# Two phase sums per group moved from ahead of the sixth to ahead of the seventh block product, from the fourth group on

## The chip, the core and the metric

The kernel runs on one core of a Trainium2 chip. The metric is the device time of one execution in microseconds (us). A run is measured as the median of its executions; one further execution is recorded by the hardware profiler, and all views of the profile below are of that one.

## What is computed

Two layers follow each other. The first is a recurrence with a complex gate per channel, over 4 batches, 8 heads, 768 steps and 48 channels; the second multiplies each of the 3072 rows by a 384 x 2048 matrix, applies h * cos(h), and multiplies by a 2048 x 384 matrix.

```python
mag = np.sqrt(a_re * a_re + a_im * a_im)
scale = np.minimum(mag, 0.999) / (mag + 1e-06)
a_re_n, a_im_n = (a_re * scale, a_im * scale)
for t in range(S):
    new_re = ar * S_re - ai * S_im          # ar, ai: gate of step t
    new_im = ar * S_im + ai * S_re
    kv = np.einsum('bhd,bhe->bhde', k[:, :, t], v[:, :, t])
    S_re, S_im = (new_re + kv, new_im)
    y[:, :, t] = np.einsum('bhd,bhde->bhe', q[:, :, t], S_re)
...
h = x @ w_in                                # x: y with the heads side by side
g = h * np.cos(h)
return (g @ w_out).astype(np.float32)
```

## The kernel before

The 768 steps of a batch are cut into 6 chunks of 128 steps, and two chunks make a group, so that there are 12 groups (0 to 11) of 256 rows. Within a chunk the recurrence becomes ordinary matrix products: the gates' magnitudes and angles are summed up along the chunk, the keys and queries are scaled by the exponentials of the sums and turned by the sines and cosines of the summed angles, and then scores, masked scores times values, and a running state give y. Summed-up angles are called phases here.

From group 2 on the function fast_path writes out one round per group n, a loop at L1541. A round mixes work of three groups. Of group n it does the scores and y (chunks, L1243), the transport of y through DRAM into the layout xT (f_x and f_xt, L1031 and L1040), and the first half of the second layer (first, L1253: eight tiles hp of two matmul groups each, with cosine and product behind each). Of group n - 1 it does the second half of the second layer. Of group n + 1 it prepares keys and queries: prods (L1226), phases (L1240) and keys (L1209).

The second half of the second layer is done, from group 2 on, by a scheme of seven block products in place of eight (seventh, L1149). Each product is eight matmuls of 128 x 192, in two parts of four. The first, fourth, sixth and seventh products add into one PSUM tile, sum, which has a single buffer; the second, third and fifth go to tiles op. After the first product ScalarE copies sum out (L1170), after the fourth VectorE adds it to an output tile (L1175), after the sixth ScalarE copies it out again, and after the seventh ScalarE copies it a last time. All these results are collected in the tiles ot. The next product that writes sum has to wait until the copy or addition of the one before has read it.

The phases of a group are two calls of g_phase (L870). Together they are six matmuls of 128 x 384 with operands hi and lo, which split the angle in two parts. Behind each call ScalarE rounds the result to whole turns (a cast to int32) and VectorE subtracts it. The step g_trig (L884) then takes two sines on ScalarE, and g_stack (L897) forms the stacked keys ks and queries qs by four products on VectorE. f_transpose (L909) transposes each in blocks of 32 on VectorE (tr), writes it to DRAM (moved, L921), and reads it back as kT by four DMAs (L924) or as qT by one (L926). The transpose of the queries is held behind the round's first gate product (gated, L919). kT and qT are what the scores of the next round read.

The order within a round is not written out. The function weave (L1196) gets lists of steps, each list with two bounds between 0 and 1; it spreads a list's steps evenly over its stretch and then runs all steps in the order of their places. TensorE's instructions are chained in exactly that order (matmul, L688), and so are the ScalarE activations that go through special and the guards on GpSimd; the remaining VectorE and ScalarE instructions and the SP queue's DMAs get their order from a scheduling layer that goes by readiness and by that same sequence. Each engine then works off its instructions in order, and all DMAs that matter here are issued from the SP queue, also in order.

With the bounds of the kernel before, the eight parts of the fourth to seventh products (products(n - 1, 3, 7), 0.4 to 0.56) stand at 0.41, 0.43 and so on to 0.55; the sixth product has 0.49 and 0.51, the seventh 0.53 and 0.55. The two phases stand at 0.473 and 0.475. keys has four steps at 0.515 (g_trig), 0.545 (g_stack and p_end), 0.575 (transpose of the keys) and 0.605 (transpose of the queries). The eight steps of first begin at 0.5875 and are 0.055 apart.

Of the kernel before, what the change touches and what calls it, by code (L numbers as in the profile page):

```python
# [487 lines left out]
def fast_path(ctx, tc, q, k, v, a_re, a_im, moe_w_in, moe_w_out, out, least, odd, wide):  # L488
# [171 lines left out]
    def behind(ins, other):  # L660
        tc.add_manual_dep(ins.ins, other.ins.name, mybir.DependencyInfo(
            mybir.DependencyClass.NoSync, mybir.DependencyReason.DATA))
# [54 lines left out]
    def spans(g):  # L717

        return [(i, 1) for i in range(G)] if g == 0 else [(0, G)]
# [116 lines left out]
    def p_end(g, i, n):  # L836
        end = X[g]["end"][:, ds(i * H, n * H)]
        vector.tensor_scalar(out=end, in0=end, scalar1=-0.5, scalar2=None, op0=ALU.mult)
        low = least[:, ds(i * H, n * H)]
        vector.scalar_tensor_tensor(out=low, in0=end, scalar=LEAST, in1=low,  # L840
                                    op0=ALU.is_ge, op1=ALU.min)
# [28 lines left out]
    def g_phase(g, i):  # L870

        x, n = X[g], g * G + i
        ps = pa.tile([C, DM], F32, tag="a", name="phs")
        early = g < PEG and n % NCH
        if not early:
            summed_up(ps, g, i, "tan", turns[0])
        else:
            matmul(ps, lhsT=turns[0], rhs=cut(x["tan"], i, 1), start=True, stop=False)
            matmul(ps, lhsT=last, rhs=before(n), start=False, stop=True)
        ph = cut(x["tan"], i, 1)  # L880
        scalar.copy(out=ph.bitcast(I32), in_=ps)
        vector.tensor_tensor(out=ph, in0=ps, in1=ph.bitcast(I32), op=ALU.subtract)

    def g_trig(g, i, n):  # L884
        x = X[g]
        if i == 0:
            x["cos"] = temp("rs")
            if g:
                x["sin"] = temp("lo")
        cs, sn = cut(x["cos"], i, n), cut(x["sin"], i, n)  # L890
        ph = cut(x["tan"], i, n)
        vector.tensor_scalar(out=cs.bitcast(U32), in0=ph.bitcast(U32),
                                scalar1=0x7FFFFFFF, scalar2=None, op0=ALU.bitwise_and)
        special(out=sn, in_=ph, func=AF.Sin, scale=TWO_PI)
        special(out=cs, in_=cs, func=AF.Sin, scale=-TWO_PI, bias=half_pi_b)

    def g_stack(g, i, n):  # L897
        x = X[g]
        if i == 0:
            for name in "ks", "qs":  # L900
                x[name] = gt.tile([C, G * H, 2, D], F32, tag=name, name=name)
        for name, product in ("ks", "Q"), ("qs", "mag"):
            for a, trig in enumerate(("cos", "sin")):
                vector.tensor_tensor(
                    out=x[name][:, ds(i * H, n * H), a],
                    in0=cut(x[product], i, n).rearrange("p (x d) -> p x d", d=D),
                    in1=cut(x[trig], i, n).rearrange("p (x d) -> p x d", d=D), op=ALU.mult)

    def f_transpose(g, i, n, name):  # L909


        if i == 0:
            X[g][name] = ft.tile([D2, G * H, Q4, 32] if name == "kT" else [D2, Q4, G * H, 32], F32,
                                 tag=name, name=name, bufs=1)
        tr = ft.tile([C, NB, n * H, 32], F32, tag="tr", name="tr")
        turn = vector.transpose(out=tr, in_=X[g][name[0] + "s"][:, ds(i * H, n * H)].rearrange(
            "p x a d -> p x (a d)").rearrange("p x (r b) -> p b x r", b=NB))
        if name == "qT" and "gated" in X[g - 1]:
            behind(turn, X[g - 1]["gated"])  # L919
        moved = rows_d.tile([Q4, D2, n * H, 32], F32, tag="moved", name="moved", bufs=3)  # L920
        nc.sync.dma_start(out=moved.rearrange("q (r b) x j -> (q r) b x j", b=NB), in_=tr)  # L921
        if name == "kT":
            for q4 in range(Q4):
                nc.sync.dma_start(out=X[g][name][:, ds(i * H, n * H), q4], in_=moved[q4])  # L924
        else:
            nc.sync.dma_start(out=X[g][name][:, :, ds(i * H, n * H)],  # L926
                              in_=moved.rearrange("q c x j -> c q x j"))
# [178 lines left out]
    PLAIN, HJ, E2 = 2, NJ // 2, DM // 2  # L1106
# [4 lines left out]
    def quarters():  # L1111

        for name in "s1", "s2", "a22":
            right[name] = stage["pool"].tile([C, HJ, E2], F32, name="t_" + name)
        t1, t2, t4 = (right[name] for name in ("s1", "s2", "a22"))
        for j in range(0, HJ, 2):
            for t, a, b in (t1, b12, b11), (t2, b22, t1), (t4, b21, t2):
                yield lambda t=t, a=a, b=b, j=j: behind(vector.tensor_tensor(
                    out=t[:, ds(j, 2)], in0=a[:, ds(j, 2)], in1=b[:, ds(j, 2)],
                    op=ALU.subtract), Y[PLAIN * G]["masked"])  # L1120

    def last_quarter():

        for j in range(0, HJ, 2):
            yield lambda j=j: vector.tensor_tensor(
                out=b12[:, ds(j, 2)], in0=b22[:, ds(j, 2)], in1=b12[:, ds(j, 2)],
                op=ALU.subtract)
# [59 lines left out]
    def products(g, lo, hi):  # L1187
        if g < PLAIN:
            return []
        return [lambda p=p, part=part: seventh(g, p, part)  # L1190
                for p in range(lo, hi) for part in range(2)]

    def mixes(g, lo, hi):
        return [lambda p=p: mixed(g, p) for p in range(lo, hi)] if g >= PLAIN else []

    def weave(*parts):  # L1196

        items = []
        for p, (part, lo, hi) in enumerate(parts):
            part = list(part)  # L1200
            items += [(lo + (hi - lo) * (i + 0.5) / len(part), p, t)
                      for i, t in enumerate(part)]
        for _, _, t in sorted(items, key=lambda x: x[:2]):
            t()
# [4 lines left out]
    def keys(g):  # L1209

        if not 0 <= g < NG:
            return
        for i, n in spans(g):
            yield lambda i=i, n=n: g_trig(g, i, n)
            yield lambda i=i, n=n: (g_stack(g, i, n), p_end(g, i, n))
            for name in "kT", "qT":
                if g >= PEG:
                    yield lambda i=i, n=n, name=name: f_transpose(g, i, n, name)
# [7 lines left out]
    def prods(g):  # L1226
        if not 0 <= g < NG:
            return
        if g not in (1, 2):
            yield from powers(g)  # L1230
            yield lambda: g_angle(g, 0, G)
        yield lambda: (g_carry(g), g_split(g))
        yield lambda: (p_even(g, 0, G), p_apply(g, 0, G))

    def logs(g):
        yield from each(g_log, g)
        if 0 <= g and g + 1 < NG:
            yield lambda: load(g + 1, ("re", "im"))

    def phases(g):  # L1240
        return [lambda i=i: g_phase(g, i) for i in range(G)] if 0 <= g < NG else []

    def chunks(g):  # L1243
        for n in range(g * G, g * G + G):
            for hh in range(2):
                yield lambda n=n, hh=hh: f_scores(n, hh)
            yield lambda n=n: f_state(n)
            yield lambda n=n: f_out(n)
        yield lambda: (f_x(g), f_xt(g))
        if g + 2 < NG:  # L1250
            yield lambda: load(g + 2, ("k", "q", "v"))

    def first(g):  # L1253
        order = range(NJ // 2) if g < PLAIN else (0, 4, 1, 5, 2, 6, 3, 7)
        return [lambda jp=jp: mm1(g, jp) for jp in order]

    def second(g, i):
        return [lambda j0=j0: mm2(g, i, j0, 4) for j0 in range(0, NJ, 4)] if g < PLAIN else []
# [282 lines left out]
    for n in range(2, NG):  # L1541
        weave((mixes(n - 1, 2, 4), 0.0, 0.12), (logs(n + 1), 0.0, 0.02), (chunks(n), 0.0, 0.36),
              (upper[2:] if n == 2 else [], 0.0, 0.2), (products(n - 1, 0, 3), 0.0, 0.36),
              (prods(n + 1), 0.25, 0.27), (second(n - 1, 1), 0.36, 0.5),
              (products(n - 1, 3, 7), 0.4, 0.56), (phases(n + 1), 0.472, 0.476),
              (keys(n + 1), 0.5, 0.62), (quarters() if n == PLAIN else [], 0.4, 0.9),
              (last_quarter() if n == PLAIN else [], 0.9, 1.0), (first(n), 0.56, 1.0),
              (mixes(n, 0, 2), 0.9, 1.0), (guarded(n - 1, per) if n > 3 else [], 0.1, 0.9))
    weave((mixes(NG - 1, 2, 4), 0.0, 0.1), (products(NG - 1, 0, 7), 0.0, 1.0))
# [76 lines left out]
```

## Time and profile before

| What | us |
|---|---|
| median of 3 runs | 666.53 |
| lowest and highest of them | 664.78 and 667.04 |
| the profiled execution's own time | 666.49 |
| its span, from the first to the last instruction | 664.7 |
| TensorE busy within it | 644.0 |
| VectorE busy | 491.7 |
| ScalarE busy | 393.3 |

The span lacks what lies before the first and after the last instruction, 1.8 us. In the views a line of a timeline gives start and length in us, engine, source line, operation, tiles (what is written, an arrow, what is read), shape, the number of instructions merged into it, and in brackets the idle time of the engine just ahead of it with the one that ended it. PE is TensorE's matmuls, PEld its weight loads, which overlap them; DVE is VectorE, ACT ScalarE, SPq the SP queue, whose lines are issues of DMAs and not the transfers. Every matmul shows up twice in the counts of such lines (x16 is a product of eight matmuls in fp32), and almost all carry the helper's line L689, so the tiles tell them apart: phs is a phase, sum and op the block products, hp the first half of the second layer, sc the scores. A row of the view of waits gives who waited for whom, the sum in us, the number of times, and the longest.

A round of groups 3 to 10 takes 51.0 to 52.3 us from one pair of phases to the next.

### The profile page before, as it was taken

To read this page: it belongs to the slowest core of one execution; us is meant where nothing else is said; L and a number is where in the kernel's file an instruction comes from. 1 tells how busy PE (TensorE), PEld (TensorE's weight loads), DVE (VectorE), ACT (ScalarE), POOL (GpSimd) and SP (SyncE) were. 2 spreads that over 40 slices of the span, in tenths; PEclk is the share of its full clock that TensorE was granted. 3 is DMA by queue.
4 is the path that set the end of the run, shared out by engine and by line. 5 is a ranking of instruction groups with operands and counts; after the bars stand their busy time and mean duration, and the time that the engine had idled before them with its cause. 6 is when DMAs were issued, how large, how long until landed. Compare 5 with 4: busy or idle time off the path is not lost.

```text
span 664.7 us, 10764 instructions
## 1 busy us (share of the span) xinstructions
PE 644.0 (97%) x4077; PEld 575.7 (87%) x4077; DVE 491.7 (74%) x797; ACT 393.3 (59%) x728; POOL 28.0 (4%) x47
## 2 busy tenths in 40 slices
PE   7899999999999999999999999999999999999995
PEld 5788867767998999899899899898899899899895
DVE  4999989499788688688688688687688778762241
ACT  7888687284673593593594494495486486332330
POOL 2010200000000000010010010000000000000000
PEclk9999999999999999999999999999999999999998
DMA  9968755637628557657648637826927833533000
GB/s 245 207 190 215 211 170 120 166 64 186 132 48 209 124 145 190 143 139 170 166 126 188 164 100 163 214 72 146 240 80 164 206 94 96 164 98 96 25 6 25
DMA packets 233626, 94.90 MB, mean 143 GB/s; under 512 B 208846, under 2 KB 222033, under 8 KB 233564
## 3 DMA queue, kind: packets, MB, share of 16 engines
q1 hardware_dynamic: 227068, 68.62, 45.2%
q0 software_dynamic: 5632, 25.17, 11.4%
q8 instruction: 34, 0.56, 0.4%
q10 hardware_dynamic: 864, 0.33, 0.2%
q14 instruction: 28, 0.23, 0.1%
HBM read 69.28 MB, written 24.81 MB: 142 GB/s over the span
## 4 chain that ended last, share of the span: by engine, by line
PE 83%; DMA 5%; ACT 5%; DVE 5%; issue 1%; POOL 0%; DVEq 0%; SPq 0%; POOLq 0%
PE hp L689 37%; PE op L689 17%; PE sum L689 11%; PE sc L689 5%; PE yp L689 5%; PE sp L689 4%; DMA xT<-x 2%; PE phs L689 2%; DMA raw<-in_moe_w_out_dram 1%; ACT rs L709 1%; DVE tan L678 1%; PE lgs L689 1%; DVE mag L678 1%; ACT lo L709 1%; DMA x<-yT 1%
## 5 line engine op out<-in xcount | busy, mean ns | idle before, releaser
L689 PE MATMUL hp<-xT,w_in 128*128 128x256 f32 (+1 forms) x1176 | 252.7, 375 | 1.4 <-DMA xT<-x 1.4
L689 PEld LDWEIGHTS hp<-xT,w_in 128*128 128x128 f32 x1176 | 219.5, 190 | 32.2 <-DMA xT<-x 2.0
L709 ACT ACTIVATE gate<-hp,half_pi_b 128x512 f32<-128x512 f32 x96 | 66.0, 687 | 120.5 <-PE hp L689 120.5
L678 DVE TENSOR_TENSOR gate<-hp,gate 128x512 f32<-128x512 f32 x96 | 65.8, 685 | 70.3 <-ACT junk L678 69.8
L689 PE MATMUL op<-w_out,gate 128*128 128x192 f32 (+1 forms) x448 | 100.7, 374 | 0.0
L689 PEld LDWEIGHTS op<-w_out,gate 128*128 128x128 f32 x448 | 75.9, 190 | 16.9 <-issue 2.0
L678 ACT ACTIVATE junk<-hp 128x512 bf16<-128x512 f32 x96 | 56.6, 590 | 0.0
L689 PE MATMUL sum<-t_s,s 128*128 128x192 f32 x320 | 55.4, 326 | 0.2 <-DVE ot L678 0.2
L678 DVE TENSOR_TENSOR atm<-sc,causal 128x512 f32<-128x512 f32 x48 | 32.8, 687 | 30.0 <-PE sc L689 30.0
L689 PEld LDWEIGHTS sum<-t_s,s 128*128 128x128 f32 x320 | 52.6, 190 | 0.5 <-DVE ot L678 0.5
L689 PEld LDWEIGHTS sc<-qT,kT 96*128 96x128 f32 x384 | 47.7, 192 | 1.9 <-ACT qT L678 0.5
L689 PE MATMUL sc<-qT,kT 96*128 96x128 f32 x384 | 49.0, 275 | 0.2 <-ACT qT L678 0.2
L678 ACT ACTIVATE ot<-sum 128x192 f32<-128x192 f32 x30 | 9.5, 319 | 45.8 <-PE sum L689 45.8
L689 PE MATMUL yp<-atm,v 128*48 128x128 f32 x352 | 33.6, 277 | 1.1 <-DVE atm L678 1.1
L705 ACT ACT_TABLE_LOAD x24 | 30.8, 1283 | 4.0 <-DMA ident<-ident_const 3.6
L678 ACT CAST tan<-phs 128x384 int32<-128x384 f32 x24 | 11.4, 480 | 36.5 <-PE phs L689 36.5
L689 PE MATMUL sum<-w_out,s 128*128 128x192 f32 x144 | 25.8, 332 | 4.2 <-ACT ot L678 4.2
L689 PEld LDWEIGHTS sp<-v,ks 128*96 128x96 f32 x320 | 29.7, 165 | 0.0
L689 PE MATMUL yp<-qT,state 96*48 96x128 f32 x304 | 29.7, 272 | 0.0
L689 PE MATMUL sp<-v,ks 128*96 128x48 f32 x320 | 29.7, 245 | 0.0
L689 PE MATMUL sum<-w_out,gate 128*128 128x192 f32 x160 | 29.6, 329 | 0.0
L689 PEld LDWEIGHTS sum<-w_out,s 128*128 128x128 f32 x144 | 23.1, 190 | 6.9 <-ACT ot L678 6.9
(138 smaller groups left out, 976.2 us busy)
## 6 DMA issues: line engine op xcount, KB each, us to landing
moved<-tr SPq DMA_DIRECT2D x20, 768.0 KB
raw<-in_moe_w_in_dram POOLq DMA_DIRECT2D x16, 768.0 KB, 5.3
raw<-in_moe_w_out_dram POOLq DMA_DIRECT2D x16, 768.0 KB, 4.9
kT<-moved SPq DMA_DIRECT2D x40, 192.0 KB
qT<-moved SPq DMA_DIRECT2D x10, 768.0 KB
k<-in_k_dram SPq DMA_DIRECT2D x24, 192.0 KB
q<-in_q_dram SPq DMA_DIRECT2D x24, 192.0 KB
v<-in_v_dram SPq DMA_DIRECT2D x24, 192.0 KB
```

The lines of the kernel that those rows point to most:

```text
L678: ins = getattr(self.engine, op)(**kw)
L689: chain(nc.tensor.matmul(out, **kw), "tensor")
L705: chain(nc.scalar.preload_act_table_set(table))
L709: chain(nc.scalar.activation(func=func, **kw))
```

## The change

In every round but that of group 2 (PLAIN is 2), the two phases of group n + 1 get the bounds 0.516 to 0.524 in place of 0.472 to 0.476, and its keys 0.53 to 0.64 in place of 0.5 to 0.62.

```diff
-              (products(n - 1, 3, 7), 0.4, 0.56), (phases(n + 1), 0.472, 0.476),
-              (keys(n + 1), 0.5, 0.62), (quarters() if n == PLAIN else [], 0.4, 0.9),
+              (products(n - 1, 3, 7), 0.4, 0.56),
+              (phases(n + 1), *((0.472, 0.476) if n == PLAIN else (0.516, 0.524))),
+              (keys(n + 1), *((0.5, 0.62) if n == PLAIN else (0.53, 0.64))),
+              (quarters() if n == PLAIN else [], 0.4, 0.9),
```

The phases then stand at 0.518 and 0.522, between the second part of the sixth product and the first part of the seventh, where they stood between the fifth and the sixth. The steps of keys come to 0.544, 0.571, 0.599 and 0.626: g_trig between the two parts of the seventh product, g_stack behind it, and the two transposes between the first and the second tile of the first layer half.

In the built program this changes eight rounds, n = 3 to 10; the round of group 11 has no further group to prepare. On TensorE only the six phase matmuls and the eight of the sixth product change places. On ScalarE the copy of sum after the sixth product moves from behind the two sines to ahead of the two casts. On VectorE the addition of op after the sixth product moves from behind the two products ks to ahead of the two phase subtractions, and in some of the rounds a small scaling, end, goes ahead of the transpose of the keys. On the SP queue the order is the same except in round 10, where the moved of the queries is issued ahead of the four kT instead of behind them. No instruction is added or removed.

## The prediction

> **What bounds the kernel now.** The page first. Its first section says that TensorE decides, and so does the chain that ended last (83% PE).
>
> ```profile
> PE 644.0 (97%) x4077; PEld 575.7 (87%) x4077; DVE 491.7 (74%) x797; ACT 393.3 (59%) x728; POOL 28.0 (4%) x47
> PEclk9999999999999999999999999999999999999998
> ```
>
> The granted clock is full throughout (0.996 in the mean), so only two things can change the time: TensorE's work, which the edit leaves alone, and TensorE's pauses. The view of waits lists those, for weight loads in the window 190:590:
>
> ```profile
> PEld sum L689 <- ACT ot L678: 6.2, 8, 0.8
> PEld lgs L689 <- DVE lo L678: 1.3, 3, 0.5
> PEld sum L689 <- DVE ot L678: 0.5, 1, 0.5
> PEld hp L689 <- DMA xT<-x: 0.5, 1, 0.5
> ```
>
> Eight waits of 0.77 us (6.2 / 8) are by far the largest item, one in each of the eight rounds n = 3 to 10 that the edit touches. Next I read one round, n = 4, in the timelines of TensorE, ScalarE, VectorE and the SP queue:
>
> ```profile
> 253.35 0.34 PE L689 MATMUL phs<-lo,exact 128*128 128x384 f32 x1
> 253.52 2.76 PE L689 MATMUL sum<-t_s,s 128*128 128x192 f32 x16
> 256.76 2.87 PE L689 MATMUL sum<-w_out,s 128*128 128x192 f32 x16 [0.48 <-ACT ot L678]
> 259.47 20.88 PE L689 MATMUL hp<-xT,w_in 128*128 128x256 f32 x96
> 280.19 1.06 PE L689 MATMUL sc<-qT,kT 96*128 96x128 f32 x8
> ...
> 256.40 0.31 ACT L678 ACTIVATE ot<-sum 128x192 f32<-128x192 f32 x1
> ...
> 250.86 0.35 DVE L678 SCALAR_TENSOR_TENSOR ot<-sum,ot 128x192 f32<-128x192 f32 x1
> 259.53 2.25 DVE L678 STREAM_TRANSPOSE tr<-ks 128x1536 f32<-128x1536 f32 x1
> 263.56 0.69 DVE L678 TENSOR_TENSOR gate<-hp,gate 128x512 f32<-128x512 f32 x1 [1.73 <-ACT junk L678]
> 264.16 2.24 DVE L678 STREAM_TRANSPOSE tr<-qs 128x1536 f32<-128x1536 f32 x1
> ...
> 261.80 4.96 SPq L921 DMA_DIRECT2D moved<-tr  x2
> 266.85 4.62 SPq L924 DMA_DIRECT2D kT<-moved  x4
> 271.58 2.66 SPq L926 DMA_DIRECT2D qT<-moved  x1
> ```
>
> Line 2 is the sixth product (eight matmuls), line 3 the seventh. Both accumulate in the same tile, sum. ScalarE copies it out between them, and TensorE stands still until that copy ends at 256.71. The phases stand just ahead of the sixth product. Below it, the path that starts at the phases: transposes on VectorE, seven DMAs on SP, and the scores of the next round at 280.19.
>
> **What the Trainium skill says.** "PSUM — Partial Sum Buffer", section "PSUM bank collisions raise a hardware error": the hardware does not hold one engine back while another uses the bank, so the program must wait. The trace agrees: the copy ends at 256.71 and the seventh product starts at 256.76. "Perfetto Trace Analysis", section "Tensor Engine Instruction (MATMUL, LD_WEIGHTS)": ScalarE and VectorE are strict FIFO, so a copy waits for all that is queued ahead of it. The trace agrees: the copy follows the sine rs (255.58 + 0.92 us) with no gap. "DMA: Bandwidth & Descriptors", section "Two DMAs through the same engine are not ordered": a DMA that reads what another wrote must wait for its completion on the issuing engine. Here this is why SP strings moved, kT and qT one behind the other.
>
> **The change part by part.** *The stall that goes.* Weight loads show the step: the sixth product's first load is at 253.35, the first load of hp at 259.31, 5.96 us apart. Two products with no pause take 2 x 2.60 (247.28 to 249.88 is one). So a round loses 0.76 us; eight rounds lose 6.0. Afterwards the six phase matmuls (252.64 + 1.06 in the chain of waits) stand in the gap. The copy starts about 0.1 us after the last matmul's modelled end, some 0.3 us into the phases, and takes 0.31: it is done with about 0.3 us to spare, and ScalarE has nothing before it (idle 3.52 us ahead of the casts). In ScalarE's new order the copy is ahead of the casts. I take the whole 0.76.
>
> *The cover that goes.* The phases now hide another read of the same tile: VectorE adds the fourth product's sum (ot<-sum,ot) before the sixth may overwrite it. Without them the sixth product wants its weights where the first phase load stands today. In rounds 4, 6, 7, 9, 10 that read ends 0.6 to 1.1 us earlier (251.21 against 252.32): nothing. In round 3 it ends at 200.64 and the load wants 200.37: 0.32 with the 0.05 of signalling. In round 5, 303.44 against 303.29: 0.20. In round 8 VectorE is late (458.82 against 457.29, where the 0.5 us DVE wait above already stands), and what follows waits for xT at 465.20 anyway: the sixth product cannot start earlier, the phases come after it, and the 0.76 buys nothing. Sum so far: 5 x 0.76 + 0.44 + 0.56 + 0 = 4.8 us.
>
> *xT.* hp also needs xT. By the arrivals of its DMA semaphore in the trace it lands ahead of hp by 1.09, 2.03, 0.55, 1.68, 0.92, 0.04, 1.61 and 5.64 us in rounds 3 to 10. With hp 0.76 earlier (0.56 in round 5) it still suffices, barely in round 5; nothing moves its issue.
>
> *What is moved.* Everything behind the phases starts 2.60 us later (one product; 2.92, 2.80 and 4.18 in rounds 3, 5, 8): two casts, two subtractions, two sines, four products, the transpose tr<-ks and the seven DMAs. One 0.35 us add (0.27 in sequence) leaves this chain, being done before. So tr<-ks in round 4 goes from 259.53 to 261.86 and ends at 264.1; the first gate product, which today starts at 263.56 after 1.73 us of idling, could then run at 262.8 but waits to 264.3; tr<-qs goes from 264.16 to 264.9. VectorE's idle time swallows most of the delay: 0.7 to 0.8 us remain in rounds 4, 6, 7, 9, 10; 1.0, 0.9 and 1.8 in 3, 5 and 8. The late gate products free hp's buffers still 0.7 us or more before they are wanted again (the second pair's, in round 8). Loads of k, q, v and the output DMAs stand ahead of moved in SP's queue and are not held back.
>
> *What is late next.* The scores need kT and qT. qT lands 1.53, 0.60, 1.14, 1.44, 1.92, 1.28, 0.70 and 1.35 us before the first score load (rounds 3 to 10, semaphore arrivals; for round 4 the DMA engines fall idle between 278 and 279). From the end of tr<-qs to that landing pass 11.6 to 13.0 us, set by issue spacing on SP and by the transfers themselves, so qT moves as tr<-qs does. The scores want to start earlier by the gain. Delay plus gain minus slack, with each round's own lag: round 3 0 (1.0 + 0.4 - 1.5), round 4 0.9, round 5 0.3, round 6 0, round 7 0, round 8 0.55, round 9 0.8, round 10 0 to 0.2. That is 2.6 us. With the mean lag of 12.3 us for all it is 1.8. I take 2.3. Bounds: 0, if qT finds emptier DMA engines by an equal amount, and 4.8 or more if kT is held up.
>
> In round 10 alone the new SP order issues both moved ahead of the four kT, as other rounds do; I count it at nothing, since qT lands at about 588.2 there and is wanted at 588.4.
>
> Net: 4.8 - 2.3 = 2.5 us less. The profiled execution took 666.49 us (span 664.7), the median shown is 666.53: both give 664.0.
>
> **The rivals.** *All of it is kept.* qT comes in time, no score waits: 666.5 - 4.8 = 661.7. For it: half of the rounds have 1.3 us of slack or more. Against: rounds 4 and 9 have 0.6 and 0.7, below even the gain of 0.76.
>
> *Given back, no difference.* The same steps with lags at their long end (13.0 us): the stalls come to about 4 us, 665.7.
>
> *The transposed keys decide, slower.* Today moved for the keys leaves at 261.80, moved for the queries 4.6 us later, and kT 5.05 after the first. Afterwards the two transposes follow each other within 3.1 us, and kT's first DMA can go only when the first moved has landed (3.2 to 3.9 us after its issue today), which is just when SP would reach it. If the two writes get in each other's way there by e us, then kT, qT and every round's scores are late by e more. The net gain is gone at e = 0.35; at 0.65 (the first landing at 4.5 us, as the slowest moved takes now) it costs 2 us net: 668.5. If VectorE's idling hid nothing, the shift of 2.3 would pass through whole and the time be near 677; the 1.73 us idle line excludes that.
>
> That the seventh product still waits is a rival inside the first step: with a late copy half of the 0.76 stays, and the result falls at 665.5 to 666.5, in the no-difference case.
>
> **How the numbers follow.** Forecast (partly given back, 662.8 to 665.3): 0.50. All kept (661.2 to 662.8): 0.20. No difference (665.3 to 667): 0.17. Slower through kT: 0.13. About 0.3%, 2.0 us, is what a measurement of this kernel tells from no change, so faster means below 664.5. That takes 0.33 of the forecast's half and all of the second case: 0.53. No difference: 0.17 of the forecast and 0.15 of the third case: 0.32. Slower: 0.13 and 0.02: 0.15. For 8 in 10 the range runs from 661.5 (all kept) to 667.0; only the slower case lies outside.
>
> **What would show it.** Right: PEld sum <- ACT ot falls from eight waits to none in rounds 3 to 10 (the last round's stays); two short PEld sum <- DVE ot waits appear in rounds 3 and 5; a new wait sc <- DMA qT, of 0.3 to 1 us, in rounds 4, 5, 8 and 9; tr<-qs about 1.5 us later than now, counted from hp's first load. Wrong: the seventh product still behind ScalarE (the copy's path is longer than 1 us), the scores waiting in all rounds (kT held), or in none (qT faster), or hp waiting for xT in more than round 8.

## The result and the profile after

The changed kernel takes 662.72 us in the median of 22 runs (659.61 to 669.49), the kernel before 665.77 us on the same chip (664.05 to 673.91, also 22 runs). The ratio is 0.995, with a 95% interval of 0.993 to 0.9971: by that ratio it is faster by 3.3 us (1.9 to 4.7), where 2.5 were forecast; the two medians differ by 3.05. Ratios, here and below, leave out the executions that fell into a slower state and are not the quotients of the medians beside them, which take in every execution. The profiled execution took 664.97 us with a span of 663.2 us.

That span is only 1.5 us shorter, and the page does not show the gain either. Its busy times by engine, and its row of the granted TensorE clock in tenths:

```profile
PE 646.2 (97%) x4077; PEld 579.2 (87%) x4077; DVE 490.6 (74%) x797; ACT 393.1 (59%) x728; POOL 28.9 (4%) x47
PEclk9979999999999999999999999999999999999999
```

TensorE is busy 2.2 us longer with the same 4077 instructions. The 7 in the third slice goes with it: from 37.1 us on the clock was granted at half for 6.8 us, ahead of all that the change touches, and just before that TensorE had begun a pause of 1.84 us for VectorE. The first weight load of hp in round 2 starts at 160.64 us, 4.5 us later than in the kernel before (156.12), although both issue the same up to that point. A span is therefore the wrong measure for this change. I use instead the stretch from the first weight load of hp in round 2 to that in round 10, read from the timelines of the weight loads, and call it the eight rounds: it holds the eight places that the change edits. It is 412.42 us before and 406.99 after.

The view of waits for weight loads, in the window that was shown of before:

```profile
PEld sc L689 <- issue: 1.4, 3, 0.6
PEld lgs L689 <- DVE lo L678: 1.3, 3, 0.5
...
PEld yp L689 <- DVE state L678: 0.5, 2, 0.2
PEld sum L689 <- DVE ot L678: 0.3, 1, 0.3
PEld sc L689 <- DMA qT<-moved: 0.2, 1, 0.2
```

The eight waits for the copy have gone, all of them. Three rows are new. Two are on the scores, 1.6 us in four waits; the third, on yp, is matched by two waits fewer in another row of yp. Three of the score waits are put down to "issue", a wait in which the view finds no releaser. The arrivals on the DMA's semaphore name it: in rounds 4, 6, 7 and 9, the four that wait, the last piece of qT arrives 0.17, 0.04, 0.10 and 0.10 us ahead of the score load. The forecast's VectorE wait shows once, in round 3 (0.3 us).

Round n = 4 in the timelines, as before:

```profile
256.54 2.76 PE L689 MATMUL sum<-t_s,s 128*128 128x192 f32 x16
...
260.00 0.34 PE L689 MATMUL phs<-lo,exact 128*128 128x384 f32 x1
260.18 2.76 PE L689 MATMUL sum<-w_out,s 128*128 128x192 f32 x16
262.78 20.88 PE L689 MATMUL hp<-xT,w_in 128*128 128x256 f32 x96
283.90 1.13 PE L689 MATMUL sc<-qT,kT 96*128 96x128 f32 x8 [0.24 <-issue]
...
259.34 0.33 ACT L678 ACTIVATE ot<-sum 128x192 f32<-128x192 f32 x1 [5.77 <-PE sum L689]
...
265.92 2.26 DVE L678 STREAM_TRANSPOSE tr<-ks 128x1536 f32<-128x1536 f32 x1
...
268.13 0.70 DVE L678 TENSOR_TENSOR gate<-hp,gate 128x512 f32<-128x512 f32 x1
268.73 2.26 DVE L678 STREAM_TRANSPOSE tr<-qs 128x1536 f32<-128x1536 f32 x1
...
268.20 3.15 SPq L921 DMA_DIRECT2D moved<-tr  x2
271.47 4.83 SPq L924 DMA_DIRECT2D kT<-moved  x4
276.41 1.95 SPq L926 DMA_DIRECT2D qT<-moved  x1
```

The copy now runs from 259.34 to 259.67, inside the six phase matmuls, and the seventh product follows the last of them at 260.18 with no pause. The price stands at the end of the TensorE lines: the scores start at 283.90 after an idle 0.24 us. From the first hp load to the first score load pass 21.25 us here against 20.67 undisturbed, so 0.58 us are given back (the 0.24 is TensorE's own idling, the 0.58 counts from weight load to weight load). On VectorE the gate product has no idle time ahead of it any more (1.73 us before): it waits for the transpose of the keys, and tr<-qs ends 8.37 us after hp's first load, 1.26 later than before (7.11). SP's queue is served in the same order: both moved, four kT, then qT, whose arrival at 283.70 is 0.17 us ahead of the score load.

### The profile page after: what moved, and what is told of

Its sections match the earlier page's. It is cut to its first block, busy times and chain, and to the rows that moved or that the text cites. A ratio compares the mean times of both kernels' runs of the same rounds, so it can differ in the third digit from the quotient of the medians.

```text
span 663.2 us, 10773 instructions
## 1 busy us (share of the span) xinstructions
PE 646.2 (97%) x4077; PEld 579.2 (87%) x4077; DVE 490.6 (74%) x797; ACT 393.1 (59%) x728; POOL 28.9 (4%) x47
## 4 chain that ended last, share of the span: by engine, by line
PE 82%; DVE 6%; DMA 6%; ACT 2%; issue 2%; SPq 1%; POOL 0%; DVEq 0%; POOLq 0%
PE hp L689 34%; PE op L689 17%; PE sum L689 13%; PE sc L689 5%; PE yp L689 5%; PE sp L689 3%; PE phs L689 2%; DMA xT<-x 1%; DMA raw<-in_moe_w_out_dram 1%; PE lgs L689 1%; DVE mag L678 1%; DMA qT<-moved 1%; SPq L924 1%; DVE atm L678 1%; PE yr L689 1%
## 5 line engine op out<-in xcount | busy, mean ns | idle before, releaser
L678 DVE SCALAR_TENSOR_TENSOR ot<-op,ot 128x192 f32<-128x192 f32 x31 | 11.0, 355 | 36.6 <-ACT ot L678 25.6
L689 PE MATMUL op<-t_a,gate 128*128 128x192 f32 x160 | 29.0, 332 | 0.0
L678 ACT COPY yT<-yp 48x512 f32<-48x512 f32 x44 | 25.2, 573 | 4.7 <-PE yp L689 4.3
```

Source lines behind the costliest of these rows:

```text
L678: ins = getattr(self.engine, op)(**kw)
L689: chain(nc.tensor.matmul(out, **kw), "tensor")
```

## The experiments

Theory: each of the eight rounds is rid of the 0.76 us in which TensorE stood waiting for the copy, since the phases cover it; part returns as score waits, because everything behind the phases starts later and qT, the last of SP's chain, lands too late. Rivals: the gain or the waits are chance of one profile; the scores wait for kT or for SP, not for the late transpose; half the cover would do.

All runs in one table. "Eight rounds" is the measure above from the one profile; "copy" is the sum of the waits of the seventh product for the copy, and "scores" the sum of what the stretch from hp to the next scores exceeds 20.67 us in rounds 3 to 9, both from the profile (for e3_ungated the score rows of its waits, since its hp stands for another reason).

| Run | median, us | before, same chip | ratio (95%) | eight rounds | copy | scores |
|---|---|---|---|---|---|---|
| before | 665.77 | | | 412.42 | 6.2 | 0 |
| changed | 662.72 | 665.77 | 0.995 (0.993 to 0.9971) | 406.99 | 0 | 1.5 |
| e1_before_again | 668.55, one | 671.5 | | 411.54 | 6.2 | 0 |
| e2_no_copy | 663.17 | 671.5 | 0.9884 (0.9827 to 0.9941) | 405.99 | 0 | 0 |
| e3_ungated | 668.81 | 671.5 | 0.9984 (0.9948 to 1.0019) | 412.54 | 0 | 0.5 |
| e4_later | 678.74 | 671.5 | 1.0145 (1.008 to 1.0211) | 418.24 | 5.7 | 7.6 |
| e5_after_again | 665.46 | 669.41 | 0.9955 (0.9931 to 0.9978) | 407.70 | 0 | 2.0 |
| e6_first_between | 669.46, one | 669.41 | | 410.31 | 3.1 | 0.6 |
| e7_second_between | 668.03, one | 669.41 | | 409.29 | 0 | 2.4 |
| e8_halves | 679.01 | 669.41 | 1.013 (1.0078 to 1.0182) | 419.09 | 13.2 | 0 |
| e9_pool_product | 670.07 | 670.0 | 1.0 (0.9965 to 1.0034) | 411.07 | 0 | 6.0 |
| e10_after_again | 667.23 | 670.0 | 0.9955 (0.9927 to 0.9983) | 407.32 | 0 | 1.7 |
| e11_reload_early | 662.57 | 668.31 | 0.9926 (0.99 to 0.9953) | 408.55 | 0 | 0.9 |
| e12_reload_early_before | 667.95 | 668.31 | 1.0006 (0.9972 to 1.004) | 412.26 | 6.2 | 0 |

### The kernel before, once more

> The kernel before once more, for a second profile. All theories: the eight rounds from hp of round 2 to hp of round 10 take 412.4 us within 0.5 again, with eight waits of 0.77 us of the seventh product for ScalarE's copy. If the lateness of VectorE in round 8 (its wait of 3.06 us for a guard's DMA, and hp's wait for xT) belongs to the kernel, round 8 takes 51.9 us again; if it was chance, some 51.2, and another round may have it.

The eight copy waits are there again with the same 6.2 us, so they are fixed. What was not there is round 8's late VectorE: that round took 50.98 us, against 51.94 in the first profile. There VectorE had stood 3.06 us for a load of second-layer weights that one of the guards looks at; here it stood 2.0 us, and TensorE did not feel it. VectorE's waits in 440:466, first profile and second:

```profile
DVE raw L678 <- DMA raw<-in_moe_w_out_dram: 3.1, 1, 3.1
...
DVE raw L678 <- DMA raw<-in_moe_w_out_dram: 2.0, 1, 2.0
```

It is no rare accident either. Over all fourteen profiles VectorE stands 2.6 us or more for this load in six (before, e3, e6, e8, e11, e12), and in those six the sixth product of round 8 waits for VectorE; in the other eight it stands 2.0 us or less, and the sixth product does not wait. Undisturbed, the eight rounds of before take 411.5 us, and this is what the others are held against.

### The stall alone

The order of before; ScalarE's copy of sum after the sixth product is left out in groups 2 to 10, so the output quarter c22 lacks that term and gets the scaled op alone.

```diff
-        if p in (0, 2, 5) or p == 6 and not alone:
+        if p in (0, 2) or p == 5 and g in (1, NG - 1) or p == 6 and not alone:
             scalar.mul(out={0: c11, 2: c21, 5: c22, 6: c12}[p], in_=ps, mul=scale)
...
+        if p == 5 and g < NG - 1:
+            added = vector.tensor_scalar(out=c22, in0=x["op"], scalar1=scale, scalar2=None, op0=ALU.mult)
...
```

> The order of the kernel before, but the copy of sum behind the sixth product is left out: the quarter of the output rows that it feeds gets the term of op alone, written by the same VectorE instruction. Theory (the gain is the seventh product's wait for this copy): the eight waits vanish with nothing moved, the eight rounds fall from 412.4 to about 407 us (8 x 0.76 less some 0.5 to 1 us for xT and qT in rounds 5, 8, 4, 9), the time to about 661. Rival (the gain came from the new order on VectorE or ScalarE): 412 and 666, unchanged.

411.54 less 405.99 is 5.6 us (6.4 against the first profile): the stall is worth what was read from it, 8 x 0.76 = 6.0, and it sits on the path that sets the end. No score waits, since the chain behind the phases has kept its start. What is lacking to the 6.0 is 0.4 us of two waits of hp:

```profile
PEld hp L689 <- issue: 0.4, 2, 0.3
```

They are in rounds 5 and 7, where xT lands 0.10 us ahead of hp's load.

### The transpose of the queries without its gate

```diff
-        if name == "qT" and "gated" in X[g - 1]:
-            behind(turn, X[g - 1]["gated"])
```

> The changed kernel, and the transpose of the queries no longer held behind the first gate product. Theory (1.5 us are given back because qT lands late): tr<-qs starts 0.6 us earlier, qT lands as much earlier, the waits of the scores (0.58 in round 4, 0.2 in 6 and 7, 0.5 in 9) fall to about 0 to 0.2 in all, and the eight rounds go from 407.0 to about 405.7 us, the time to about 661.5. Rival (the first gate product, now 2.25 us later, holds hp's PSUM buffer): waits of hp for VectorE appear and the eight rounds take 407 us or more.

The main expectation failed and the rival held: the ratio to before can't be told from 1. Waits of the weight loads, then VectorE and TensorE in round 4:

```profile
PEld hp L689 <- DVE gate L678: 4.8, 7, 0.7
```

```profile
264.95 2.25 DVE L678 STREAM_TRANSPOSE tr<-qs 128x1536 f32<-128x1536 f32 x1
267.13 1.24 DVE L678 TENSOR_TENSOR gate<-hp,gate 128x512 f32<-128x512 f32 x2
...
259.59 7.93 PE L689 MATMUL hp<-xT,w_in 128*128 128x256 f32 x36
267.83 13.22 PE L689 MATMUL hp<-xT,w_in 128*128 128x256 f32 x60 [0.31 <-DVE gate L678]
```

tr<-qs now runs ahead of the first gate product, so that product ends late, the buffer of hp's first tile comes free late, and hp stands 0.4 to 0.6 us in the middle of each round (mostly 21.24 us to the scores in place of 20.67). The lateness moved from the scores into hp. In this profile VectorE was also late in round 8 (1.6 us of the 412.54); without that the eight rounds are 410.9, against 411.5 of before.

### The phases still later

The phases between the two parts of the seventh product, so that the copy has no cover and everything behind them starts one part later again.

```diff
-              (phases(n + 1), *((0.472, 0.476) if n == PLAIN else (0.516, 0.524))),
+              (phases(n + 1), *((0.472, 0.476) if n == PLAIN else (0.536, 0.542))),
```

> The phases once more later, between the two parts of the seventh product. Theory (cover gone, and lateness passes through to the scores now that VectorE's idle time is used up): the eight waits of 0.7 us for the copy are back (about 6 us), and the scores wait for qT 1.3 us more in most rounds (1.5 us in all now, some 7 then): eight rounds about 418 to 419 us, time about 674 to 676 on the scale of 666 before. Rival (the lateness is still swallowed by idle time): only the 6 us come back, 412.5 to 413 us, time 667.

It holds: 418.24 us. The waits show both halves of it.

```profile
PEld sc L689 <- issue: 6.9, 6, 1.8
PEld sum L689 <- ACT ot L678: 5.7, 8, 0.7
...
PEld sc L689 <- DMA qT<-moved: 1.0, 1, 1.0
```

The further shift is 1.3 us, and tr<-qs ends 9.5 us after hp's first load where it ended 8.4: VectorE's idle time, which swallowed much of the first shift, is used up, and from here on the scores pay for lateness. The copy waits are 0.71 us each and not 0.77. Here, as in the changed kernel, the copy starts 0.04 us after the sixth product's modelled end; in the kernel before it starts 0.12 us after it, behind the sine. So 0.06 to 0.08 us of the old wait came from the sine queued ahead of the copy, and the rest from the copy and its hand-over. In this run, too, qT lands between 0.04 and 0.2 us ahead of every score load that waits, so the "issue" rows are waits for qT.

### One phase on each side

The cover split. In the one variant only the first phase (two matmuls) stands between the sixth and the seventh product, in the other only the second (four). The edit of the first variant:

```diff
+              (phases(n + 1) if n == PLAIN else phases(n + 1)[1:], 0.472, 0.476),
+              ([] if n == PLAIN else phases(n + 1)[:1], 0.516, 0.524),
```

> Of the two phases only the first, two matmuls and about 0.35 us, stands between the sixth and seventh product; the second (four matmuls, 0.70 us) is back ahead of the sixth. Theory (what counts is the length of the work that covers the copy, which needs about 0.75 us): eight waits of about 0.4 us for the copy, half of the gain: eight rounds of about 409 us. Rival (any change of tile between the two products is enough, or the copy is just ordered better on ScalarE): 407, or 411.5.

> Only the second phase, four matmuls and about 0.70 us, stands between; the first is ahead of the sixth. Theory: the cover is just too short or just enough, eight waits of 0 to 0.1 us; round 3 loses its wait of 0.3 us for VectorE's addition; the scores wait as long as in the changed kernel: eight rounds of 406.7 to 407.5 us. Rival of e6: as there.

With two matmuls (0.35 us of TensorE) each of the eight waits shrinks from 0.77 to 0.39 us:

```profile
PEld sum L689 <- ACT ot L678: 3.1, 8, 0.4
```

With four (0.70) the view counts none. But the seventh product's first load stands 0.05 us behind the copy's end in all eight rounds, as it does where it waits, against 0.34 in the changed kernel: 0.70 us is just at the edge. So the cover counts by its length, needs to be some 0.75 us long, and the second phase alone would nearly do. It does not gain over both: its score waits are 2.4 us. The wait that the cover takes from VectorE's read of the fourth sum (0.3 us, once) is not there in the second variant, where two matmuls remain ahead of the sixth product. Both are single profiles, and both contain a lateness of VectorE that not every profile has (1.5 us in round 8 of the first, 1.3 in round 9 of the second), so I read the waits and not their totals.

### The sines and products by halves

To win back the score waits, group halves: the first half's phase ahead of the sixth product, with its sines and products while that runs, the second half's phase between. The edit also ties ScalarE's copy to a place behind the first half's sines, and VectorE's addition after the sixth product to one behind the first half's products.

```diff
...
+              (phases(n + 1)[:1], 0.472, 0.476), (phases(n + 1)[1:], *((0.472, 0.476) if n == PLAIN else (0.516, 0.524))),
+              ([] if n == PLAIN else part_keys(n + 1, 0), 0.48, 0.5), ([] if n == PLAIN else part_keys(n + 1, 1), 0.525, 0.55),
...
```

> As e7, and the sines and products behind each phase are done for each half by itself, the first half's on ScalarE ahead of the copy and on VectorE ahead of the last addition, while the sixth product runs. Theory (1 to 1.5 us are given back because the transposes stand 0.7 us too late behind the phases): tr<-qs starts about 1.1 us earlier against hp than in the changed kernel, the scores wait for nothing, and the eight rounds come to 406.0 to 406.8 us, the time 0 to 1 us below the changed kernel's. Rival (the half-size steps cost as much in fixed time as they gain, or the first sines hold the copy up): waits for the copy or for qT stay, 407 us or more.

It failed: the wait for the copy doubled (13.2 us, 1.7 each). TensorE's, ScalarE's and VectorE's lines of round 4:

```profile
261.98 2.87 PE L689 MATMUL sum<-w_out,s 128*128 128x192 f32 x16 [1.33 <-ACT ot L678]
...
260.69 0.52 ACT L709 ACTIVATE lo<-tan 128x384 f32<-128x384 f32 x1 [2.82 <-PE phs L689]
...
261.62 0.31 ACT L678 ACTIVATE ot<-sum 128x192 f32<-128x192 f32 x1
...
260.34 0.36 DVE L678 TENSOR_SCALAR rs<-tan 128x384 uint32<-128x384 uint32 x1 [1.88 <-PE phs L689]
```

The cosine's tile shares its buffer with hi, and the sine's with lo, which the second phase's matmuls still read. So the first half's step rs on VectorE waits for them, the sines behind it stand, as the edit has it, in ScalarE's queue ahead of the copy, and the copy starts 1.67 us after the sixth product's modelled end in place of 0.04. Of the idea itself, apart from the shared buffers, this run says nothing; it was not tried with buffers of its own.

### A product on GpSimd

```diff
-                vector.tensor_tensor(
+                eng = nc.gpsimd if name == "qs" and a == 0 and g > PLAIN + 1 else vector
+                eng.tensor_tensor(
```

> The changed kernel, and from the preparation of group 4 on one of the four products of g_stack, qs<-mag,rs, on GpSimd in place of VectorE. It takes 0.95 us of VectorE ahead of tr<-qs in each round. Theory (what is given back of the gain is the lateness of tr<-qs, and nothing else): tr<-qs starts up to 0.9 us earlier, unless GpSimd's product itself ends later than that; the score waits of 1.5 to 2.0 us in rounds 4, 6, 7 and 9 nearly vanish; the eight rounds take 405.5 to 406.5 us against 407.0 to 407.7 of the changed kernel, the time is 0 to 1.5 us below it. Rival (GpSimd is too slow, or slows VectorE while both work): qs is complete only after more than 3 us from the sines, tr<-qs waits for GpSimd by name, and the score waits grow; eight rounds of 408 us or more.

The rival held. The two products of the queries in round 4, on VectorE and on GpSimd:

```profile
263.65 2.57 DVE L678 TENSOR_TENSOR qs<-mag,lo 128x768 f32<-128x768 f32 x1
...
262.85 2.55 POOL L905 TENSOR_TENSOR qs<-mag,rs 128x768 f32<-128x768 f32 x1 [16.89 <-ACT rs L709]
```

GpSimd needs 2.55 us for what VectorE does in 0.95, and VectorE's own product beside it takes 2.57. It ends 0.8 us after GpSimd's, so it did nearly all of its work only once GpSimd was done (the profile's spans on GpSimd are rough). The Trainium skill says so in "SBUF — State Buffer", section "SBUF: two separate sides": the two engines share a pair of ports that works as an exclusive lock for an instruction with two SBUF inputs. The trace agrees. GpSimd's 2.55 us may hold a wait of the same kind: when it starts, at 262.85, VectorE has just begun the product ahead, ks<-Q,rs (262.78 to 263.73); this is not shown apart. tr<-qs comes later by 0.8 us against its own hp, not earlier by 0.9, and the score waits grow to 6.0 us, where the changed kernel has 1.5 to 2.0: lateness of the queries, whatever makes it, reaches the scores.

### The changed kernel again

> The changed kernel once more. All theories: eight rounds of 407 us within 0.5, no wait for the copy in rounds 3 to 10, waits of the scores for qT of 1 to 2 us in all, which may fall on other rounds than 4, 6, 7 and 9. Against the kernel before on the same chip a ratio of 0.992 to 0.996.

> The changed kernel again, beside the variant with GpSimd's product on the same chip. Theory: the ratio to the kernel before is 0.993 to 0.998, the eight rounds take 406.5 to 408 us, no wait of the seventh product for the copy, and score waits of 1 to 2.5 us in all, most of them in rounds 4, 6 and 9. A rival (the gain belongs to the chips of the first runs): a ratio that holds 1.

Two different chips give 0.9955 both times. The score waits vary in place and size (0.55, 0.65, 0.18 and 0.60 us in rounds 4, 6, 7 and 9 of the one, 0.29, 0.18, 0.46 and 0.74 in the other); the rounds are the same.

### The reload of the queries ahead of the last of the keys

In the changed kernel qT, wanted as the last, is issued last, while kT's fourth part lands 4.2 us ahead of its use in round 4.

```diff
-            for q4 in range(Q4):
+            X[g]["moved"] = moved
+            for q4 in range(3 if g > PLAIN + 1 else Q4):
                 nc.sync.dma_start(out=X[g][name][:, ds(i * H, n * H), q4], in_=moved[q4])
         else:
...
+            if g > PLAIN + 1:
+                nc.sync.dma_start(out=X[g]["kT"][:, ds(i * H, n * H), 3], in_=X[g]["moved"][3])
```

> The changed kernel, and from the preparation of group 4 on the one DMA that reloads qT is issued behind the third of the four that reload kT, not behind the fourth. In the changed kernel the fourth kT lands 4.2 us and more ahead of the scores (2.6 in one round), qT last, and the queries' moved has landed 1.8 us before qT is issued (round 4). Theory (the give-back is the lateness of qT, and SP's queue is part of it): qT is issued and lands 1.2 to 1.4 us earlier, kT's fourth part lands 1.5 to 2.5 us later and still ahead of the scores; the score waits of 1.5 to 2.0 us go to 0.3 or less; eight rounds of 405.3 to 406.3 us against 407.0 to 407.7, the ratio to before 0.990 to 0.994. Rival (the transfers share engines, so that qT's bytes only push kT's aside): kT's last part is what the scores now wait for, the waits stay at 1 us or more, eight rounds of 407 us or more.

> The kernel before with the same reordering of the reloads alone. Its scores wait for nothing (qT lands 0.6 us and more ahead of them). Theory: it gains nothing, eight rounds of 411.3 to 412.5 us as before, eight waits of the seventh product for the copy, ratio 0.998 to 1.002; so an effect in the other run belongs to the two edits together. Rival (reloads in another order relieve other transfers as well): eight rounds below 411 us and a ratio below 0.997.

SP's queue of the first (changed kernel and reload), then the waits of its weight loads:

```profile
267.03 3.70 SPq L925 DMA_DIRECT2D kT<-moved  x3
270.84 1.04 SPq L927 DMA_DIRECT2D qT<-moved  x1
271.92 1.07 SPq L930 DMA_DIRECT2D kT<-moved  x1
```

```profile
PEld sc L689 <- issue: 0.5, 2, 0.3
...
PEld sc L689 <- DMA kT<-moved: 0.4, 1, 0.4
```

qT is issued 1.1 us earlier, counted from the end of tr<-qs (4.29 against 5.42 us in round 4), and lands 1.5 us earlier (11.24 against 12.71). The waits fall to 0.9 us, not to the expected 0.3 or less: kT's last part now lands last, 0.04 to 0.1 us ahead of the score loads in rounds 6, 7 and 9, because it takes 6 to 7 us behind qT's bytes where it took 3.6 to 5.7 in the changed kernel's three profiles. So both sides had a part. The 408.55 us of its eight rounds contain 1.8 of late VectorE in round 8 (it stood 3.0 us for the guard's load again); without that they are 406.8. Over the kernel before it gains 0.74% in the median, the largest gain besides e2's. Against the changed kernel's 0.9955 the intervals overlap, the two were timed on different chips, and 406.8 is hardly below 407.0; so that it beats the changed kernel is suggested by the shorter score waits and not shown. With the order of before, the same edit gains nothing (412.26 with 0.8 of late VectorE in round 8), as it should if what it saves exists only once the scores wait.

## Why the prediction was right

Forecast and result are 664.0 and 662.72 us; the gain was forecast as 2.5 and measured as 3.3 (1.9 to 4.7). By rounds, with the undisturbed before (e1) as the base; "saved" is the stretch from the scores to hp, measured in the changed kernel's first profile; the three values of the score wait are its three profiles:

| Round | saved, forecast | saved, measured | score wait, forecast | score wait, measured |
|---|---|---|---|---|
| 3 | 0.44 | 0.48 | 0 | 0, 0.04, 0.04 |
| 4 | 0.76 | 0.73 | 0.9 | 0.58, 0.55, 0.29 |
| 5 | 0.56 | 0.73 | 0.3 | 0, 0, 0 |
| 6 | 0.76 | 0.76 | 0 | 0.21, 0.65, 0.18 |
| 7 | 0.76 | 0.86 | 0 | 0.23, 0.18, 0.46 |
| 8 | 0 | 0.85 | 0.55 | 0, 0, 0 |
| 9 | 0.76 | 0.73 | 0.8 | 0.50, 0.60, 0.74 |
| 10 | 0.76 | 0.87 | 0 to 0.2 | 0, 0, 0 |
| sum | 4.8 | 6.0 | 2.6, taken 2.3 | 1.5, 2.0, 1.7 |

*The stall that goes.* Right in kind, place and size: none of eight is left, and e2 prices them at 5.6 us. The copy had the time that was forecast for it, 0.3 us to spare; e6 and e7 show where the cover ends, at some 0.75 us. That the copy waits behind the sine, which the forecast read off the missing gap, is true but worth no more than 0.08 us a round: the sixth product itself ends at nearly the same time.

*The cover that goes.* Right for round 3 (0.3 us forecast and seen, in all three profiles). Round 5's 0.20 did not come. Round 8's zero was the largest mis-sized term: it took one profile's late VectorE, and the late xT behind it, for a fixture. e1 and the three profiles of the changed kernel don't have the wait for VectorE, and there the round saves 0.85, 0.52 and 0.86. The reasoning for that round was sound where the lateness does come: with the phases gone from ahead of the sixth product, that product waits 1.5 us for VectorE in e3 and e11, against 0.5 and 0.3 in before and e12, and the round is 1.6 and 1.8 us longer, not 1.0 and 0.8. So the change makes this lateness dearer, which the three profiles of the changed kernel do not show.

*What is moved.* The shift of 2.3 us to tr<-ks came out as computed: in round 4 it went from 0.22 to 3.30 us after hp's first load, 3.08, of which 0.76 is hp's own earlier start. The gate's 1.73 us of idling swallowed the rest as said. tr<-qs then came 1.26 us later against hp and not 1.5, since it starts 2.81 us after tr<-ks; the forecast had put 3.04 between them.

*What is late next.* Right in kind: the scores wait for qT, in some rounds only. The size was 2.3 and measured 1.5 to 2.0. The lags from tr<-qs to qT's landing were taken from one profile per round; they move by up to 0.8 us from profile to profile (round 5: 11.15, 11.95 and 11.95 us in the changed kernel). Rounds 6 and 7, counted at nothing, wait, and rounds 5 and 8 don't. A lag with that scatter gives a sum and no list of rounds; that the sum came near with two rounds missed and two too many is in part luck.

*xT.* It suffices nearly everywhere. In round 5, which was called barely enough, it lands 0.04 us ahead of hp's load in the changed kernel's first profile; hp waits 0.3 us in round 8 of e5 and in round 5 of e10. The wait in round 5 is one that the forecast had named as a sign of being wrong; it is small and in one profile of three.

*The rivals.* All kept: refuted, there are score waits in every profile. kT held up: the first moved lands 3.25 us after its issue in round 4, 3.26 before, so the two writes do not hinder each other; kT is 4.2 us early. That it can be brought to decide, e11 shows. A late copy: refuted.

The two mis-sized terms, 1.0 to 1.2 us of saving too little and 0.3 to 0.8 of give-back too much, go the same way: the three profiles save 6.0, 5.8 and 5.9 us and give back 1.5, 2.0 and 1.7, and the eight rounds give 3.8 to 4.6 (411.54 less 407.70, 407.32 and 406.99). That is within the interval of the timed runs, above its middle. So the mechanism was right and the gain was forecast too small by 1.3 to 2.1 us; that the timed gain, 3.3, lies nearer to 2.5 than the rounds do is luck, or due to something that the profiles do not show.

## What to carry to other kernels

Where one PSUM buffer is written, read out and written again, put independent matmuls between: what counts is that their length reaches that of the read-out with its hand-over (here some 0.75 us), and what they covered before must be looked at too. Moving the head of a long chain costs only what the idle time along it does not swallow, so add up that chain to its last transfer; and once the last transfer decides, the order of the queue that issues it is worth another look. Before one profile's stall is booked as fixed, or its absence in a second one as proof of chance, take several profiles: round 8's came in six of fourteen.

## What the runs showed that was not expected

*Most of the scatter goes with the clock.* Within one kernel on one chip the time falls by 0.77 us for each 0.001 of mean granted clock (correlation -0.89 over the timed runs of these experiments), and with that taken out the standard deviation falls from 2.7 to 1.2 us. At a clock of 0.996 the differences from before become -3.8 and -4.0 us for the changed kernel (each within 0.8), -6.4 for e2 (1.3), -0.6 for e3 (0.7), +8.3 for e4 (1.6), +7.6 for e8 (1.1), -0.8 for e9 (1.0), -4.5 for e11 (0.7) and -0.1 for e12 (0.6). For all but e4 these agree with the eight rounds of the profiles better than the plain medians do. This is a correlation; the next paragraph shows a pause that comes with a cut of the clock and costs time of its own.

*The start varies with one late DMA.* The first hp load of round 2 stands between 155.89 and 162.31 us in the fourteen profiles; kernels that are the same up to there fall on both ends (156.17 in e11, 162.31 in e10). Six profiles have it at 156.2 or earlier, eight at 159.0 or later. In the eight, VectorE waits 2.6 to 3.6 us near 37 us for the DMA end<-row (0 to 0.9 in the six), TensorE then stands 1.2 to 2.3 us for VectorE's state, and the granted clock falls to half for 3.4 to 10.2 us. The six have no such pause and no cut there. The pause begins ahead of the cut in all eight; that it brings the cut about is not shown.

*Two engines, one product each.* The 0.95 us product of VectorE took 2.57 us beside GpSimd's.
